# A re-planned DeltaNet and SwiGLU kernel: weight tile sums, masks and K transposes on other engines

## The chip, the cores and the metric

The kernel runs on one core of a Trainium2 chip. Its engines are TensorE (PE in the profile, with PEld for its weight loads), VectorE (DVE), ScalarE (ACT), GpSimd (POOL) and SyncE (SP), which here only issues DMAs. The metric is the device time of one execution in microseconds; three runs of the kernel before gave 681.6, 685.14 and 685.31 us.

## The reference

Two blocks in a row. The first is a DeltaNet recurrence over 768 steps for 4 batches of 8 heads of 48 elements; the second is a feed-forward block with RMS norm over 3072 tokens of 384 elements, 1536 wide inside.

```python
k_n = k / (np.linalg.norm(k, axis=-1, keepdims=True) + 1e-06)
for t in range(S):
    kt, vt, bt = (k_n[:, :, t], v[:, :, t], beta[:, :, t, None])
    y[:, :, t] = np.einsum('bhd,bhde->bhe', q[:, :, t], state)
    v_old = np.einsum('bhde,bhd->bhe', state, kt)
    state = state + bt[:, :, :, None] * np.einsum('bhd,bhe->bhde', kt, vt - v_old)
...
xn = x / np.sqrt(np.mean(x * x, axis=-1, keepdims=True) + 1e-06) * rms_g
g = xn @ w_gate
out = (g * (1.0 / (1.0 + np.exp(-g))) * (xn @ w_val)) @ w_out
```

All is float32, except that the three weight matrices arrive as 64-bit floats and are converted on the chip.

## The kernel before

**Tiling.** The 768 steps are cut into 12 chunks of 64 steps. A chunk holds 256 tokens (4 batches of 64). For each chunk the kernel inverts the coupling of the 64 steps among themselves, so that the recurrence becomes a few matmuls per chunk, and then runs the feed-forward block over the chunk's 256 tokens. The parts are:

- `load`, `norms`, `prep16` (chunks 0 and 1) and `prep` (from chunk 2): K is loaded, normalised (squares on ScalarE at line 665, sum on VectorE, power on GpSimd at 669, scaling of K on GpSimd at 738 or 897), turned on TensorE (`turn`, 621) and multiplied with itself (`scores`, 644). The inverse of the coupling is worked out in small steps on VectorE (816 and 822 for chunks 0 and 1, 977 and 983 later). In `prep` the scores go through DRAM into another layout (`dkk`, `dx`), are scaled on GpSimd (930, 955, 960) or, for chunks 2 and 3, on VectorE, and are put together by two groups of matmuls (1032, 1052).
- `qpart`: Q is turned (on TensorE for chunks 0 and 1, by a transpose on VectorE of a squared layout in `q2` afterwards, 652), multiplied with K (644), and the scores are masked on VectorE into `pt` (689).
- `recur`: the state times K and times Q (`on_state`, 1091, each a group of 64 products on half the rows of the array), then for chunks 0 and 1 the products 1165 and three rounds of 1177 with ScalarE and VectorE between them, and for later chunks one group 1151; then the output (1187) and the state's change (1256). A norm (line 1293, power at 1306) and a transposition (1338, or `dyn` in DRAM and 1329 from chunk 4 on) give the feed-forward block its input.
- `ffn_plain` for chunks 0 and 1 (1405 up, 1387 down); `ffn` from chunk 2 on uses fewer products of sums of operands (1498, with evacuations at 1508, 1510, 1514 and 1515; 1555 down), for which VectorE first works out factors of the weights (1463, 1534).
- `weights`: 18 tiles of 768 KB are loaded into three landing buffers `raw`. ScalarE (561) and VectorE (549, 552, 557) make two parts of each tile, which are added: for the first two tiles (`NPE = 2`) on TensorE, by an identity product of each part into one bank (573, 574) and a copy out on ScalarE (578); for the others by one VectorE add (581).

**Order.** All operations are handed to a planner, `Plan`. It has a duration for each, walks forward and backward over the graph several times (`ROUNDS`, `SEEDS`), and emits the instructions of each engine in the order of its best walk. Operations made while `P.first` is set (the first chunk's preparation and recurrence) have priority over all others. `due(c, lead)` gives the other operations their wanted times, 51 us per chunk. `RELEASE` holds the earliest times of the first weight loads. Until 70 us `filler` puts products of the identity (1664) into TensorE's planned pauses; `supply` models the fetching of TensorE's instructions. There are eight PSUM banks of 128x512, taken and freed in the planned order. TensorE takes products in program order, so one that waits holds up all behind it. Nearly all DMAs are issued on SP's queue by one helper (427).

The masks that the score products are multiplied with:

```python
P.add("DVE", 0.72, lambda d=d, dst=dst: nc.vector.tensor_tensor(
    out=dst, in0=heads(ps[d]), in1=mask_p[:, None, :].to_broadcast([128, 8, C]), op=ALU.mult,
), pr, r=[ps[d], "mask"], w=[("pt", d)], last=ps[d])
```

The way of K through DRAM that `prep` already holds, but never takes, since `KSQ` is 99:

```python
dma(dsq, kn.rearrange("p x e -> p (x e)"), pn, r=kkeys + kp, w=["dsq"], dur=0.6, work=1.4)
for z in range(4):
    src = dsq.rearrange("(gh t) (u z e) -> z t u gh e", t=32, z=4, e=32)[z]
    dst = q2[32 * z : 32 * z + 32].rearrange("p x e -> p (x e)").rearrange("p (u gh e) -> p u gh e", u=8, gh=4)
    dma(dst, src, pn, r=["dsq"], w=q2k[4 * z : 4 * z + 4], work=0.8)
square_turn(kt[ikq], ktk, pr)
```

Of the kernel before, what the change touches and what calls it, by code (L numbers as in the profile page):

```python
# [14 lines left out]
ALU = mybir.AluOpType  # L15
# [3 lines left out]
C = 64  # L19
# [6 lines left out]
ROUNDS, SEEDS = 200, (3,)  # L26
# [3 lines left out]
EARLYN = ()  # L30
RELEASE = (4.7, 13.0, 22.0, 25.0, 30.0, 33.0, 36.0)
KSQ, XSQ = 99, 4
DRAIN, REFILL, GRACE = 0.1, 0.2, 0.0
SHAKE = 0.12
SPARE = 1.0


class Op:
    def __init__(self, eng, dur, fn, prio, deps, lat, acquire, release, slack):
        self.eng, self.dur, self.fn, self.prio = eng, dur, fn, prio  # L40
        self.lat, self.acquire, self.release, self.slack = lat, acquire, release, slack
        self.deps, self.users, self.left = sorted(deps, key=lambda d: d.n), [], len(deps)
        self.mode = None
        self.ready, self.dma, self.ahead, self.work = 0.0, False, 0.0, 0.0
# [24 lines left out]
class Plan:  # L69
# [47 lines left out]
    def forward(self, banks, until):  # L117
# [11 lines left out]
        order, server, end_, mode = [], 0.0, 0.0, 0  # L129
        self.lag = 0.0  # L130
        count, asked, usable = 0.0, -9.0, {}

        def supply(s, dur, n0, size, keep):

            late, last, got = 0.0, asked, {}
            for k in range(int(n0) // BLOCK, int(n0 + size) // BLOCK + 1):
                for mark in (ASKED, LACKED):
                    n = BLOCK * k + mark
                    if not n0 < n <= n0 + size:
                        continue  # L140
                    t = s + late + dur * (n - n0) / size
                    if mark == ASKED:
                        last = max(t + max(REACT, min(server - t + 1.2, 3.5)), last + TURN)
                        got[k + 1] = last + LAND
                    else:
                        late += max(0.0, got.get(k, usable.get(k, 0.0)) - t)
            if keep:
                usable.update(got)
            return late, last
        lanes = [0.0] * 8  # L150
        while len(order) < len(self.ops):
            best = None
            for e in ENGINES:
                for op in cand[e]:
# [12 lines left out]
                    if op.size:  # L167
                        seen += supply(s, op.dur, count, op.size, False)[0]
                    if best is None or (seen, key, op.n) < best[0]:
                        best = (seen, key, op.n), op, s  # L170
# [3 lines left out]
            cand[op.eng].remove(op)  # L174
            for g in op.acquire:
                if not g.taken:
                    g.taken = True
                    free.pop(0)
# [108 lines left out]
def kernel(  # L287
# [58 lines left out]
    NPE, NRAW, NCV = 2, 3, 2  # L346
# [165 lines left out]
    def weights(n0, n1):  # L512
# [14 lines left out]
        for n, (dst, src, keys) in list(enumerate(todo))[n0:n1]:  # L527
# [38 lines left out]
            if n < NPE:  # L566
                width = 768 // parts
                for x_, (a0, a1) in enumerate(((0, 2), (2, 3)) if parts == 3 else ((0, 1), (1, 2))):
# [7 lines left out]
                    P.add("PE", 0.2 + 0.0018 * m, s6, pr, r=cvk + cak + ["ident"], w=[("cvp", n, x_)], ps=ps, size=8)  # L576
# [11 lines left out]
    def load(c, what):  # L588
# [8 lines left out]
        for key, t, src, pr in (("k2", k2[c % NK], k, pk), ("q2", q2, q, pq)):  # L597
            for g in range(2):
                if key[0] not in what or key == "q2" and c > 1:
                    continue  # L600
                dst = t[64 * g : 64 * g + 64, :, 0:D]
                s = src.rearrange("b (y g) t e -> g t (b y) e", g=2)[g, t0 : t0 + C]
                op = dma(dst, s, pr, w=[(key, c % NK, g)] if key == "k2" else q2k[8 * g : 8 * g + 8], dur=0.7, work=1.02, eng="ACT" if c == 0 and g and key == "k2" else "SP", after=((0.0, 12.0, 0.0), (2.2, 40, 0.0))[c]["kqv".index(key[0])] if c < 2 else 44.5)
                op.lat += LATE if c == 1 or key == "q2" else 0.0
# [62 lines left out]

# [9 lines left out]
    def qpart(c):  # L677
# [9 lines left out]
        for d in range(2):  # L687
            dst = pt[:, d:16:2]
            P.add("DVE", 0.72, lambda d=d, dst=dst: nc.vector.tensor_tensor(
                out=dst, in0=heads(ps[d]), in1=mask_p[:, None, :].to_broadcast([128, 8, C]), op=ALU.mult,  # L690
            ), pr, r=[ps[d], "mask"], w=[("pt", d)], last=ps[d])


    def spread_scores(ps, pr, split):
        for d in range(2):
            out_ = scor[:, :, d:16:2].rearrange("p t u -> p u t")
            if split and d == 0:
                P.add("DVE", V(512), lambda o=out_, d=d: nc.vector.tensor_scalar_mul(o, heads(ps[d]), -1.0), pr, r=[ps[d]], w=[("sp", d)], last=ps[d])
            else:
                P.add("ACT", A(512), lambda o=out_, d=d: nc.scalar.mul(o, heads(ps[d]), -1.0), pr, r=[ps[d]], w=[("sp", d)], last=ps[d])  # L700

    def prep16(c):
# [43 lines left out]
        for j in range(3):  # L746
            cut = slice(L * j, L * j + L)
            P.add("ACT", A(256), lambda j=j, cut=cut: nc.scalar.mul(under[:, :, cut], scor[:, cut].rearrange("p t x -> p x t"), below[:, j : j + 1]), pd + (12 if c == 0 else 1), r=[("sp", 0), ("sp", 1), "below"], w=["under"])
# [58 lines left out]
        P.add("DVE", V(128), share1, pi, r=ab, w=xkeys)  # L807
        P.add("DVE", 0.3, share3, pi, r=ab, w=ak)
        P.add("DVE", V(128), share2, pi, r=xkeys, w=ab)
# [27 lines left out]
        P.add("ACT", 0.65, spread, pi, r=ak, w=xkeys)  # L837
# [231 lines left out]
    def recur(c):  # L1069
# [11 lines left out]
        if c:  # L1081
# [27 lines left out]
            P.add("PE", 0.98, lambda: (on_state if c > 1 else on_state_rows)(kt[ikq], psk), pr, r=ktk + sk, w=psk + rk, ps=psk, size=128)  # L1109
# [12 lines left out]
            P.add("PE", 0.98, lambda: on_state(qt, psq), pr, r=qk + sk, w=psq, ps=psq, size=128)  # L1122
# [490 lines left out]
    prep16(0)  # L1613
    qpart(0)
    P.first = False
# [84 lines left out]
```

## Time and profile before

| what | value |
|---|---|
| median of 3 runs | 685.14 us (681.6 to 685.31) |
| the profiled execution | 687.73 us, of it span 686.0 us |
| mean granted TensorE clock | 0.994 |
| VectorE, ScalarE, GpSimd busy | 548.1, 306.5, 137.1 us |
| feed-forward products, chunks 2 to 11 (1498) | 2400 records, 177.2 + 125.9 us |
| their evacuation by adds (1508) | 180 of 682 ns |
| transposes of K on TensorE (621) | 96 records, 13.7 us |
| masks on VectorE (689) | 24, 15.8 us |
| DMA | 58.10 MB, mean 85 GB/s |

The span runs from the first to the last instruction. The profile counts two records for each float32 product, and one for a transposition. Busy times are unions of spans; the spans of matmuls overlap, so that a pause on TensorE is better seen in the starts of its products. A row of the timeline gives the start, the length, the engine, the line, the tiles and the count, and in brackets the idle time of the engine before it and what ended it.

### The profile page before, as it was taken

The page shows a single profiled execution, that of the slowest core. Times are in us where ns is not written, and L with a number is a line of the kernel's source. Part 1 is how long each engine was busy: PE and PEld are TensorE (multiplying, and loading weights), DVE is VectorE, ACT ScalarE, POOL GpSimd, SP SyncE. Part 2 cuts the span into 40 slices and gives each one's busy share as a digit, 9 for nine tenths or more (in the row PEclk, how much of TensorE's full clock was granted, in tenths as well). Part 3 has the DMA queues.
Part 4 walks back from the last instruction along what each step waited for, and adds up shares of the span by engine and source line. Part 5 has one row for each costly group of instructions (what it writes and reads, how often), then busy time and mean ns, then how long its engine had stood idle before and what let it go on. Part 6 is the DMA issues. An engine that isn't in the chain of part 4 may idle for free.

```text
span 686.0 us, 23536 instructions
## 1 busy us (share of the span) xinstructions
PE 667.7 (97%) x10076; PEld 613.7 (89%) x10076; DVE 548.1 (80%) x1153; ACT 306.5 (45%) x717; POOL 137.1 (20%) x142
## 2 busy tenths in 40 slices
PE   7798999999999999999999999999999999999997
PEld 4576778878799999999999999999999999999997
DVE  5749999999989789669888789689689799457473
ACT  6367452434245445336346346256345444253340
POOL 3202030104312312123222222222231301000000
PEclk9899999999999999999999999999999999999999
DMA  8549774614521643643634633643635435002101
GB/s 146 166 109 211 188 229 94 140 26 76 84 49 26 101 71 75 107 80 64 106 58 78 104 66 78 100 82 65 100 60 92 72 79 79 15 12 47 24 1 24
DMA packets 244953, 58.10 MB, mean 85 GB/s; under 512 B 232304, under 2 KB 237424, under 8 KB 244848
## 3 DMA queue, kind: packets, MB, share of 16 engines
q1 hardware_dynamic: 243808, 56.40, 42.6%
q8 instruction: 79, 1.29, 0.8%
q10 hardware_dynamic: 1040, 0.20, 0.2%
q14 instruction: 26, 0.21, 0.1%
HBM read 42.14 MB, written 14.42 MB: 82 GB/s over the span
## 4 chain that ended last, share of the span: by engine, by line
PE 88%; DVE 5%; ACT 2%; issue 2%; DMA 1%; SPq 1%; DVEq 0%; ACTq 0%
PE bank L1498 37%; PE bank L1555 20%; PE bank L1405 8%; PE bank L1387 5%; PE bank L1091 3%; PE bank L644 3%; PE bank L621 2%; PE bank L1187 2%; PE bank L1151 1%; PE bank L1177 1%; SPq L427 1%; DVE tmp L1508 1%; PE bank L1256 1%; PE bank L1032 1%; PE bank L1052 1%
## 5 line engine op out<-in xcount | busy, mean ns | idle before, releaser
L1498 PE MATMUL bank<-xf,w_in 128*128 128x128 f32 x1440 | 177.2, 276 | 0.3 <-ACT tmp L1510 0.3
L1498 PEld LDWEIGHTS bank<-xf,w_in 128*128 128x128 f32 x1440 | 168.7, 192 | 1.8 <-ACT tmp L1510 0.5
L1508 DVE TENSOR_TENSOR tmp<-tmp,bank 128x512 f32<-128x512 f32 x180 | 121.1, 682 | 41.0 <-PE bank L1498 32.3
L1498 PE MATMUL bank<-xf,more 128*128 128x128 f32 x960 | 125.9, 278 | 1.8 <-DVE tmp L1508 1.4
L1498 PEld LDWEIGHTS bank<-xf,more 128*128 128x128 f32 x960 | 115.2, 192 | 4.8 <-DVE tmp L1508 2.0
L1510 ACT COPY tmp<-bank 128x512 f32<-128x512 f32 x120 | 68.9, 585 | 77.0 <-PE bank L1498 60.8
L1514 ACT ACTIVATE tmp<-tmp 128x256 f32<-128x256 f32 x120 | 49.6, 417 | 86.0 <-DVE tmp L1508 85.7
L983 DVE TENSOR_REDUCE acc<-acc 128x30 f32<-128x90 f32 (+4 forms) x150 | 70.9, 473 | 5.2
L669 POOL TENSOR_TENSOR knrm<-ksum,half 128x16 f32<-128x16 f32 x12 | 36.3, 3028 | 166.1 <-DVE ksum L668 166.1
L1555 PE MATMUL bank<-wo_sb,hf 128*128 128x192 f32 x360 | 64.1, 328 | 0.0
L977 DVE TENSOR_TENSOR acc<-acc,at 128x60 f32<-128x60 f32 (+4 forms) x150 | 52.0, 347 | 12.3 <-DMA out_dram<-tmp 4.4
L1555 PEld LDWEIGHTS bank<-wo_sb,hf 128*128 128x128 f32 x360 | 58.3, 190 | 0.4
L1515 DVE TENSOR_TENSOR hf<-tmp 128x256 f32<-128x256 f32 x120 | 48.8, 421 | 9.6 <-ACT tmp L1514 8.5
L930 POOL TENSOR_TENSOR at<-at,beta_b 128x1024 f32<-128x1024 f32 x8 | 19.1, 2384 | 127.4 <-DMA at<-dkk 78.4
L1405 PE MATMUL bank<-xf,w_in 128*128 128x256 f32 x144 | 33.8, 386 | 0.0
L1387 PE MATMUL bank<-wo_sb,hf 128*128 128x384 f32 x96 | 33.7, 490 | 0.0
L1405 PE MATMUL bank<-xp,w_in 128*128 128x256 f32 x144 | 32.8, 380 | 0.0
L1564 DVE TENSOR_TENSOR tmp<-tmp,bank 128x192 f32<-128x192 f32 x30 | 10.5, 350 | 26.4 <-PE bank L1555 26.4
L1405 PEld LDWEIGHTS bank<-xp,w_in 128*128 128x128 f32 x144 | 27.0, 190 | 4.9
L1003 POOL COPY acc<-acc 128x128 f32<-128x128 f32 x40 | 18.1, 480 | 63.3 <-DVE acc L983 62.9
L1405 PEld LDWEIGHTS bank<-xf,w_in 128*128 128x128 f32 x144 | 26.6, 190 | 4.5 <-issue 0.4
L1357 DVE TENSOR_TENSOR xf<-xf 128x256 f32<-128x256 f32 (+1 forms) x70 | 25.1, 396 | 2.6 <-ACT xf L1331 2.0
(203 smaller groups left out, 1030.0 us busy)
## 6 DMA issues: line engine op xcount, KB each, us to landing
at<-dkk SPq DMA_DIRECT2D x20, 256.0 KB, 3.9
more<-in_moe_w_gate_dram SPq DMA_DIRECT2D x6, 768.0 KB, 5.7
vt<-in_v_dram SPq DMA_DIRECT2D x24, 192.0 KB, 4.0
more<-in_moe_w_val_dram SPq DMA_DIRECT2D x6, 768.0 KB, 6.0
more<-in_moe_w_out_dram SPq DMA_DIRECT2D x6, 768.0 KB, 5.1
out_dram<-tmp SPq DMA_DIRECT2D x48, 96.0 KB, 2.2
k<-in_k_dram SPq DMA_DIRECT2D x23, 192.0 KB, 4.1
dyn<-yn SPq DMA_DIRECT2D x16, 192.0 KB, 1.9
```

The source lines that it names most:

```text
L669: P.add("POOL", 2.95, lambda: nc.gpsimd.tensor_tensor(out=knrm[i2], in0=ksum[i2], in1=half, op=ALU.pow), pn, r=[("ksum", i2), "half"], w=[ ...
L977: nc.vector.tensor_tensor(out=acc[:, 1:3, 0:n, j + 2 : W].rearrange("p a i t -> p i a t"), in0=acc[:, old, 0:n, j : j + 2, None].to_broadc ...
L983: nc.vector.tensor_reduce(out=acc[:, new, 0:n, j + 2 : W], in_=acc[:, lo : lo + 3, 0:n, j + 2 : W].rearrange("p a i t -> p i t a"), axis=A ...
L1357: P.add("DVE", V(128 * n), lambda dst=dst, a=a, b_=b_, op=op: nc.vector.tensor_tensor(out=dst, in0=a, in1=b_, op=op), pxv, r=[("xp", 0)], ...
L1387: nc.tensor.matmul(po[p].t[:, 0:DM], hf[:, spot(f), 128 * p : 128 * p + 128], wo_sb[:, spot(f)], start=(f == f0), stop=(f == f1 - 1), skip ...
L1405: nc.tensor.matmul(ps.t[:, TOK * side : TOK * side + TOK], w_in[:, side, h_, 3 * t + i_, n : n + 128], x_[:, 2 * t : 2 * t + 2].rearrange( ...
L1498: nc.tensor.matmul(g.t[:, 128 * z : 128 * z + 128], fac[:, side, 128 * f : 128 * f + 128], xf[:, xs], start=(begin and z == 0), stop=False ...
L1508: P.add("DVE", V(512), lambda t=t, g=g: nc.vector.tensor_tensor(out=t, in0=t, in1=g.t, op=ALU.add), -1, r=[g], w=[tk], last=g)
L1510: P.add("ACT", A(512), lambda t=t, g=g: nc.scalar.copy(t, g.t), -1, r=[g], w=[tk], last=g)
L1514: P.add("ACT", A(256), lambda t=t: nc.scalar.activation(out=t[:, 0:256], in_=t[:, 0:256], func=ACTF.Silu), -1, w=[tk])
L1515: P.add("DVE", V(256), lambda t=t, f0=f0, p=p: nc.vector.tensor_tensor(out=hf[:, spot(f0) : spot(f0) + 2, 128 * p : 128 * p + 128], in0=t[ ...
L1555: nc.tensor.matmul(g.t[:, 0:192], a_[:, f], b_[:, f], start=(begin and f == 0), stop=(f == 5), skip_group_check=True)
```

## The change

The planner gets new rules and constants:

- In a walk after the first, each operation of the first chunk's chain remembers when it started in the walk before. Another operation that would still run at that time on the same engine (with an allowance of 0.1 us) is put behind it.
- The first chunk's Q (`qpart(0)`) is no longer part of that chain.
- The model of instruction fetches also counts the DMA queue before 100 us; several planned durations are changed; fillers leave 0.5 us free, not 1.0; 100 rounds with another seed.

And the kernel does some steps otherwise:

- `NPE = 0`: no tile sums on TensorE; all 18 tiles are added on VectorE.
- `EARLYN = (3, 4)`: weight tiles 3 and 4 land in the space of `hf`, not in `raw`; the loads of tiles 1 to 3 are released at 10, 13 and 16 us, not 13, 22 and 25.
- Both loads of the first Q are issued on ScalarE's queue from 1.4 us on, not on SP's from 12 us on.
- `JKQ = 3`: from chunk 3 on the state's products with K and with Q are one operation of the plan, with four banks.
- `KSQ = 8`: the K of chunks 8 to 11 goes through DRAM into `q2` and is turned by VectorE, not by TensorE.
- `POOLM = 2`: from chunk 2 on ScalarE copies the two banks of Q's scores into `pt`, and GpSimd zeroes what the mask excludes, in two instructions of 64 rows.

```diff
-ROUNDS, SEEDS = 200, (3,)
+ROUNDS, SEEDS = 100, (1,)
...
-EARLYN = ()
-RELEASE = (4.7, 13.0, 22.0, 25.0, 30.0, 33.0, 36.0)
-KSQ, XSQ = 99, 4
+JKQ, JMR, JSC = 3, 99, 99
+EARLYN = (3, 4)
+RELEASE = (4.7, 10.0, 13.0, 16.0, 30.0, 33.0, 36.0)
+KSQ, XSQ = 8, 4
+POOLM = 2
...
-SPARE = 1.0
+SPARE = 0.5
+KEEP, SOON = 0.1, 100.0
...
+        chain = {e: [] for e in ENGINES}
+        for op in self.ops:
+            op.was, op.done = op.start, False
+            if op.first and op.was is not None:
+                chain[op.eng].append(op)
+        for e in ENGINES:
+            chain[e].sort(key=lambda op: -op.was)
...
+                        if t < SOON:
+                            last = max(last, min(server - 0.7, last + 4.5))
...
+                while chain[e] and chain[e][-1].done:
+                    chain[e].pop()
+                kept = chain[e][-1].was + slip if chain[e] else 1e9
...
+                    if not op.first and seen + op.dur - KEEP > kept:
+                        seen = max(seen, kept)
...
+            op.done = True
+            if op.first and op.was is not None:
+                slip = s - op.was
...
-    NPE, NRAW, NCV = 2, 3, 2
+    NPE, NRAW, NCV = 0, 3, 2
...
-                op = dma(dst, s, pr, w=[(key, c % NK, g)] if key == "k2" else q2k[8 * g : 8 * g + 8], dur=0.7, work=1.02, eng="ACT" if c == 0 and g and key == "k2" else "SP", after=((0.0, 12.0, 0.0), (2.2, 40, 0.0))[c]["kqv".index(key[0])] if c < 2 else 44.5)
+                op = dma(dst, s, pr, w=[(key, c % NK, g)] if key == "k2" else q2k[8 * g : 8 * g + 8], dur=0.7, work=1.02, eng="ACT" if c == 0 and (g or key == "q2") else "SP", after=((0.0, 1.4, 0.0), (2.2, 40, 0.0))[c]["kqv".index(key[0])] if c < 2 else 44.5)
...
+            if c < POOLM:
+                P.add("DVE", 0.72, lambda d=d, dst=dst: nc.vector.tensor_tensor(
+                    out=dst, in0=heads(ps[d]), in1=mask_p[:, None, :].to_broadcast([128, 8, C]), op=ALU.mult,
+                ), pr, r=[ps[d], "mask"], w=[("pt", d)], last=ps[d])
+                continue
+            P.add("ACT", A(512), lambda d=d, dst=dst: nc.scalar.copy(dst, heads(ps[d])), pr, r=[ps[d]], w=[("pt", d)], last=ps[d])
+        for g in range(2) if c >= POOLM else ():
+            rows = slice(64 * g, 64 * g + 64)
+            P.add("POOL", 1.9, lambda rows=rows: nc.gpsimd.affine_select(
+                out=pt[rows], in_=pt[rows], pattern=[[0, 16], [1, C]], compare_op=ALU.is_gt, fill=0.0, base=0, channel_multiplier=-1,
+            ), pr, w=ptall)
+            P.ops[-1].port = False
...
-            P.add("PE", 0.98, lambda: (on_state if c > 1 else on_state_rows)(kt[ikq], psk), pr, r=ktk + sk, w=psk + rk, ps=psk, size=128)
+            if c < JKQ:
+                P.add("PE", 0.98, lambda: (on_state if c > 1 else on_state_rows)(kt[ikq], psk), pr, r=ktk + sk, w=psk + rk, ps=psk, size=128)
+            else:
+
+                def both_states():
+                    on_state(kt[ikq], psk)
+                    on_state(qt, psq)
+
+                P.add("PE", 1.96, both_states, pr, r=ktk + qk + sk, w=psk + psq + rk, ps=psk + psq, size=256)
...
-    qpart(0)
     P.first = False
+    qpart(0)
```

## The prediction

> **What bounds the kernel now.** I read the page's busy line first, then the table of windows, then the chain of waits from 27 to 57 us, then the timeline there.
>
> The page's busy line, share of the span in brackets:
>
> ```profile
> PE 667.7 (97%) x10076; PEld 613.7 (89%) x10076; DVE 548.1 (80%) x1153; ACT 306.5 (45%) x717; POOL 137.1 (20%) x142
> ```
>
> Matmuls overlap, so 97% alone proves little. The windows (sum, then busy time of PE, PEld, DVE, ACT, POOL, clock, DMA share, GB/s) show where PE has room:
>
> ```profile
> 30.00:40.00 10.00, 8.39 (x128) 5.79 (x131) 2.46 (x6) 2.74 (x7) 0.00 (x0) 0.83 0.72 151
> 40.00:50.00 10.00, 10.00 (x317) 8.25 (x310) 5.58 (x12) 7.92 (x17) 0.00 (x0) 1.00 0.16 22
> 50.00:60.00 10.00, 8.27 (x128) 6.69 (x119) 9.38 (x29) 9.02 (x28) 1.80 (x2) 1.00 1.05 231
> 140.00:150.00 10.00, 10.00 (x142) 7.84 (x130) 9.79 (x20) 3.35 (x9) 0.00 (x0) 1.00 0.02 5
> 340.00:390.00 50.00, 50.00 (x824) 48.65 (x823) 41.55 (x88) 23.69 (x57) 11.49 (x14) 1.00 0.47 82
> ```
>
> After 190 us TensorE alone binds: VectorE has 8.5 of 50 us free. From 50 to 187 us TensorE and VectorE are both full. From 30 to 50 us VectorE works 8.0 of 20 us and the DMA engines drop to 22 GB/s, although nine weight tiles have to be loaded and converted then. The chain of waits (start, length, what) says why:
>
> ```profile
> 27.76 1.85 PE bank L1165 x64
> 30.09 1.60 issue
> 32.03 1.18 PE bank L573 x2
> 33.21 1.71 PE bank L574 x2
> 34.92 1.39 PE bank L1664 x4
> 36.30 2.00 PE bank L1177 x64
> ```
>
> L1165 and L1177 are the first chunk's recurrence. [...] The timeline shows the second such place, and the first feed-forward matmul:
>
> ```profile
> 43.52 0.30 ACT L1214 COPY u<-bank 128x192 f32<-128x192 f32 x1
> ...
> 46.37 1.07 PE L1177 MATMUL bank<-state,wsum 64*64 64x48 f32 x29
> ...
> 56.53 4.15 PE L1405 MATMUL bank<-xf,w_in 128*128 128x256 f32 x18
> ```
>
> From L1405 on TensorE hardly pauses. So two things can move the end: when L1405 starts, and how much TensorE work follows it.
>
> **The change part by part.**
>
> *Tile sums off TensorE, kept times.* In the built program's order no filler or tile sum stands between these products any more; 22 fillers, for 18, fill other waits. The half-1 values of L1165 were copied out by 30.36 (the timeline's DVE copy L1216, 30.00 + 0.36), and half 0 could have started at 29.6, yet L1177 began at 36.23: 6.6 us lost. At the second place u was ready at 43.82 (43.52 + 0.30) and L1177 began at 46.37: 2.55 lost. Together 9.2 us. The 1.6 us "issue" I cannot tie to the sums, so the gain is 7.6 to 9.2; I take 7.6, since nothing in the diff removes that stall. On VectorE the two sums cost 2 x 0.97 us (the row of L581), inside the 12 us it has idle from 30 to 50; if that cover were gone they would delay the conversions by 1.9.
>
> *What ScalarE pays.* Q of chunk 0 is now issued on ScalarE's queue, ahead of the activation that makes K's squares. K's own issue there took 0.73 us; two are 1.46, less the 0.35 that ScalarE waited for K anyway: +1.1 at the head of the chain. Three things there give it back: the scores of Q (L644, 1.1 us) stood between coupling and L1165 and now sit where fillers stood; a conversion step (L549, 0.57) stood ahead of the diagonal blocks (L854); and Q leaves SP's queue ahead of the weights, where its two issues took 5.16 us. I count this start as 0, with -1 to +1.5. Between the recurrence and L1405, however, the new order puts all three `under` products (L748, 0.73 each) and a 0.37 us copy of chunk 1 before the last scaling of the activations; ScalarE was 90% busy from 50 to 60 us, so about 1.5 us of these lie on the path (0 to 2.6).
>
> So L1405 starts 7.6 - 1.5 = 6.1 us earlier (bounds 9.2 + 1.0 = 10.2 and 7.6 - 1.5 - 2.6 = 3.5).
>
> *Whether the weights follow.* Tiles 3 and 4 get their own landing space in `hf`, and releases move from 22 and 25 to 13 and 16 us, into the slot of 22 GB/s. By the order four tiles are converted before the first feed-forward product; in the trace tile 3 got its last add at 58.52, after L1405. So VectorE stands at the new, earlier L1405 at least where it stood at 56.5. The new wait, that the gated product (L1413) may write `hf` only after tile 3 is read, ends long before.
>
> *Moved behind L1405.* Q of chunk 1: eight transposes (0.87 us at the pace below) and its scores (1.1), 2.0 in all. They partly fill the wait for L867, idle 1.87 us in the trace: I take +1.1 (0 to 2.0).
>
> *Late K by VectorE.* From 459.60 L1498 runs 10.02 us and goes on at 470.49 (rows of the chain): eight transposes take 0.87. Four chunks save 3.5 us of TensorE, and ScalarE eight copies of 0.59. Added per chunk are a store and four loads on SP and a transpose on VectorE (L652, 1.24 us). SP's five issues cost some 2.5 us at the 0.5 of its neighbours; queued behind them are sixteen loads of Q, which share `q2`, and `dyn`/`yn`. Latency: store 1.9, issues 2.0, landing 3.0 (the `dyn` rows), transpose 1.24: 8 us for what took about 2. It is covered while K is early: K's pair of loads issued at 359.79 belongs to a norm whose power starts at 408.86, so K lies ready for tens of us. Price: -3.5, if covered.
>
> *K and Q products as one group.* A lone group of 64-row products costs about 0.33 us beyond its own time (by the starts in the trace the pitch before it is 0.09 longer, the two after it 0.13 and 0.10). Nine joins could save 3.0. But in the built order the feed-forward stage from L1498 on is broken by 55 such groups, before and after: other neighbours were parted. From L1405 on it is 72 against 69, so +1.0 (bounds -3.0 and +1.0). The group now waits for K, Q and state and takes four banks at once, as L1187 with L1256 already does; products of L1498 are queued behind it and L1117 waits for it.
>
> *Mask by GpSimd.* VectorE loses 20 x 0.68 = 13.6 us, ScalarE gets 20 copies of 0.59 = 11.7, GpSimd 20 selects. No row has a select that large: 64x64 took 0.26 us, a memset of 128x1024 1.0, a two-input product of 128x1024 2.38. I take about 1.1 (select and memset both read at most one input), bounds 1.0 and 2.4. On GpSimd's queue they stand ahead of the scalings of K and of the scores (L897, L930), 2.2 us per chunk where it idles 38 of 50. ScalarE and VectorE have room after 190 us too, and the masked scores are wanted only by L1187: 0 on the path, unless GpSimd stops VectorE (a rival below).
>
> Sum: -6.1 + 1.1 - 3.5 + 1.0 = -7.5 us. The profiled execution took 687.73 (span 686.0 and 1.73 around it) and should become 680.2; the median of the runs shown, 685.14, lies 2.6 below it, which gives **677.6 us**.
>
> [...] Two rows bear on sharing between GpSimd and VectorE:
>
> ```profile
> 172.07 0.68 DVE L1463 TENSOR_TENSOR more<-w_in 128x512 f32<-128x512 f32 x1
> ...
> 182.15 4.93 DVE L1463 TENSOR_TENSOR w_in<-w_in 128x512 f32<-128x512 f32 x2
> ```
>
> The same sum takes 0.68 us alone and 2.46 while GpSimd runs a two-input product. Beside GpSimd's one-input copies (L1003) no VectorE instruction was longer than its usual by over 0.22. [...]
>
> **The rivals.**
>
> 1. *VectorE is the bound from 50 to 187 us and the early start is lost there.* For: it is over 98% busy from 120 to 150, and the feed-forward stage of chunk 2 needs all factors. Against: it brings its idle 12 us forward and loses 2 x 2 masks (2.7 us) in this stretch. Then only late K and the switches count: 685.1 - 3.5 + 1.0 = 682.6.
>
> 2. *GpSimd's selects stop VectorE.* Two chunks' selects fall where VectorE is full: 4 x 2.4 = 9.6 us, less the 2.7 saved, is 6.9: 677.6 + 6.9 = 684.5. Against: the L1003 row.
>
> 3. *Late K comes late (slower).* The 8 us path has SP's queue in it, where ten loads of Q took 5.64 us at 342.71. If K lands behind them, TensorE, in order, stands at the scores of K with everything queued behind. 8 + 5.6 - 2 = 11.6 later per chunk, less the 2.7 us between K's scaling (363.44 + 1.65) and its turn at 367.8 that the trace left, is 8.9; over four chunks 35.6: 713. It decides once K's store is issued less than about 8 us before the scores' slot; 13.6 us (8 + 5.6) ahead it would cost nothing even behind Q.
>
> 4. *The grouping does nothing.* By the switch counts I already take it so; were all nine joins real, 677.6 - 4.0 = 673.6.
>
> **How the numbers follow.** A change under 1% (6.9 us) could hardly be told from none, so faster means under 678.3 and slower over 692.0. Forecast (rival 4 within it) 0.68, rival 1 0.14, rival 2 0.08, rival 3 0.10. The forecast's own bounds: 685.1 - 10.2 - 3.5 - 3.0 = 668.4 and 685.1 - 3.5 + 2.0 - 3.5 + 1.0 = 681.1. The centre lies just below the limit, so of 0.68 I give 0.48 to faster and 0.20 to same; rivals 1 and 2 are same. Faster 0.48, same 0.42, slower 0.10. The range must reach rivals 1 and 2: 669 to 685.
>
> **What would show it.** First L1405-type matmul near 50 us, not 56.5; no tile sums; VectorE over 6 of 10 us busy from 30 to 50; 0.87 us gone from the four late K turns, and no TensorE idle before those scores; 20 selects near 1.1 us. It is wrong if the first feed-forward product starts after 53 us, if TensorE idles for weights between 60 and 100 us by more than the 3.2 us it does now (1.87 before L867, 1.32 of "issue" before L644), or if single gaps over 1 us open after 350 us.

## The result, and the profile after

In twenty runs of each, the changed kernel took 686.56 us (median; 684.33 to 695.49) and the kernel before 684.04 (681.48 to 687.48): a ratio of 1.0036, 95% interval 1.0020 to 1.0052. The forecast was 677.6 us, in a range of 669 to 685. By the medians the change costs 2.5 us; it was to save 7.5.

The two profiled executions lie at opposite ends of their kernels' runs: before 687.73 us, after 684.6. Taken by themselves they show a gain. So the kernel before was profiled a second time; that execution took 681.7 (span 680.0). Its windows from 20 to 40 us (sum, busy time of PE, PEld, DVE, ACT, POOL, granted clock, DMA share, GB/s), and the timeline where the feed-forward block begins:

```profile
20.00:30.00 10.00, 7.60 (x214) 6.93 (x215) 9.61 (x21) 5.00 (x12) 5.02 (x2) 1.00 0.51 176
30.00:40.00 10.00, 10.00 (x241) 8.28 (x240) 3.70 (x10) 5.53 (x12) 0.00 (x0) 1.00 0.81 158
```

```profile
51.28 1.16 PE L644 MATMUL bank<-qt,kt 64*64 64x64 f32 x64
52.37 1.99 PE L1405 MATMUL bank<-xf,w_in 128*128 128x256 f32 x8
```

The granted clock, 0.83 from 20 to 40 us in the first profile, is 1.00 here, and the first feed-forward product starts at 52.37, not 56.53. The 4.2 us belong to that execution, not to the program. The comparisons below use this second profile of before, unless they name both.

The changed kernel's page, its windows, and the timeline at its first feed-forward product:

```profile
PE 659.3 (97%) x10036; PEld 607.3 (89%) x10036; DVE 551.5 (81%) x1139; ACT 311.5 (46%) x725; POOL 161.6 (24%) x162
```

```profile
30.00:40.00 10.00, 9.74 (x303) 8.47 (x301) 9.75 (x23) 6.63 (x19) 0.50 (x1) 1.00 0.55 132
40.00:50.00 10.00, 8.76 (x128) 6.61 (x127) 7.43 (x20) 9.07 (x21) 1.55 (x2) 1.00 0.95 195
50.00:60.00 10.00, 9.31 (x166) 7.83 (x164) 9.19 (x20) 6.72 (x17) 1.55 (x1) 1.00 0.34 88
340.00:390.00 50.00, 50.00 (x830) 48.54 (x830) 38.06 (x80) 25.21 (x59) 9.80 (x10) 1.00 0.50 92
390.00:440.00 50.00, 47.04 (x727) 44.99 (x730) 42.96 (x89) 19.66 (x48) 14.98 (x16) 1.00 0.50 93
440.00:490.00 50.00, 47.94 (x774) 46.40 (x767) 40.54 (x89) 23.11 (x55) 15.25 (x15) 1.00 0.54 100
```

```profile
45.55 1.35 PE L1701 MATMUL bank<-ident 128*128 128x512 f32 x4
46.74 1.47 PE L1442 MATMUL bank<-xf,w_in 128*128 128x256 f32 x6
```

Read them from the top. The early start is there: L1442 (L1405 before) starts at 46.74, 5.6 us earlier. VectorE works 17.2 of the 20 us from 30 to 50, where the two profiles of before had 8.0 and 11.6, and the DMA engines move 195 GB/s from 40 to 50 us, where they had moved 22 and 132. But from 390 us on TensorE is no longer full: 47.04 and 47.94 of 50 us, where before it had 50.00. VectorE lost 13.6 us of masks and got two tile sums (1.9 us) and four transposes of K (5.0); from the 548.1 and 555.0 us of the two profiles of before, 541 to 548 were due, and it is busy for 551.5. Something may have made its instructions longer; as those two profiles differ by 7 us themselves, this is a hint and no more.

The accounting that the rest of this document uses is worked out from the starts of TensorE's products in each trace. The span is the start of the first feed-forward product, plus the stretch from there to the last product, plus a tail of 4.4 to 4.9 us. In the stretch, every step from one product to the next that is over 0.3 us longer than the clean pace of that product is a pause; filler products are counted apart; the rest is work.

```text
kernel          first product  pauses  of these after 200 us  fillers  work   span
before, 2nd     52.4            3.7     1.3                   0        619.3  680.0
after           46.7           13.2     9.2                   0        617.9  682.9
```

The parts of a row, with the tail, fall short of the span by up to 0.5 us. So -5.6 from the start and -1.4 of work are outweighed by +9.5 of pauses, nearly all of them (+7.9) after 200 us. The waits of TensorE after 186 us (total us, times, longest) say what they end on; after first, then before:

```profile
PE bank L1535 <- DVE tmp L1545: 6.1, 7, 1.6
PE bank L1119 <- issue: 1.4, 1, 1.4
PE bank L1060 <- DMA m1bd<-dxt: 0.3, 1, 0.3
```

```profile
PE bank L1498 <- DVE tmp L1508: 0.6, 2, 0.4
PE bank L1498 <- issue: 0.3, 1, 0.3
PE bank L1498 <- ACT tmp L1510: 0.3, 1, 0.3
```

TensorE waits for the evacuation L1545 on VectorE. The chain of waits ahead of the longest of these pauses (396.5 us) shows why VectorE is late, although it has 7 of 50 us to spare there:

```profile
383.32 3.69 DMA at<-dkk
...
387.18 2.35 POOL at L958
...
389.59 1.76 POOL acc L983
...
391.84 1.31 POOL at L988
...
393.17 1.14 DVE acc L1005
...
394.62 0.95 DVE acc L1005
...
397.66 0.59 DVE tmp L1545
```

The planner put four pairs of inversion steps (L1005, L1011) ahead of the evacuation. The steps need GpSimd's three scalings (L958, L983, L988), and these need `at`, which two DMAs bring from DRAM. SP's timeline (start, length of the issues) shows eight other issues between the two:

```profile
377.82 0.50 SPq L447 DMA_DIRECT2D at<-dkk  x1
378.37 4.42 SPq L447 DMA_DIRECT2D mt<-dx  x7
382.83 0.45 SPq L447 DMA_DIRECT2D q<-in_q_dram  x1
383.32 0.50 SPq L447 DMA_DIRECT2D at<-dkk  x1
```

So the evacuation, whose products had ended by 396.74 us, stood in VectorE's order behind steps whose data came late: the four pairs run from 393.17 to 397.66, and L1545 starts at 397.58, as the last of them ends. The room was in the engine but not in its order. The late data alone don't make this pause, though: the run with small selects below has the same steps, equally late, in the same place, and TensorE doesn't stand there.

### The profile page after: what moved, and what is told of

Read it like the earlier page. It is cut to its first block, busy times and chain, and to the rows that moved or that the text cites. A ratio compares the mean times of both kernels' runs of the same rounds, so it can differ in the third digit from the quotient of the medians.

```text
span 682.9 us, 23501 instructions
## 1 busy us (share of the span) xinstructions
PE 659.3 (97%) x10036; PEld 607.3 (89%) x10036; DVE 551.5 (81%) x1139; ACT 311.5 (46%) x725; POOL 161.6 (24%) x162
## 4 chain that ended last, share of the span: by engine, by line
PE 62%; DVE 14%; SPq 9%; DMA 7%; issue 3%; POOL 3%; ACT 1%; DVEq 0%; POOLq 0%; ACTq 0%
PE bank L1535 28%; PE bank L1592 12%; SPq L447 9%; PE bank L1442 7%; PE bank L1424 4%; DVE tmp L1545 3%; DMA at<-dkk 2%; DVE acc L1005 2%; PE bank L1119 2%; DVE acc L1011 2%; DMA beta_b<-in_beta_dram 1%; PE bank L1188 1%; DMA q<-in_q_dram 1%; PE bank L1224 1%; PE bank L664 1%
## 5 line engine op out<-in xcount | busy, mean ns | idle before, releaser
L1535 PE MATMUL bank<-xf,w_in 128*128 128x128 f32 x1440 | 181.0, 278 | 3.1 <-DVE tmp L1545 3.0
L1545 DVE TENSOR_TENSOR tmp<-tmp,bank 128x512 f32<-128x512 f32 x180 | 119.3, 681 | 46.4 <-PE bank L1535 36.5
L1535 PE MATMUL bank<-xf,more 128*128 128x128 f32 x960 | 124.4, 278 | 3.1 <-DVE tmp L1545 3.0
L1011 DVE TENSOR_REDUCE acc<-acc 128x30 f32<-128x90 f32 (+4 forms) x150 | 70.9, 472 | 5.2
L1005 DVE TENSOR_TENSOR acc<-acc,at 128x60 f32<-128x60 f32 (+4 forms) x150 | 56.7, 378 | 10.3 <-POOL at L988 7.6
L1552 DVE TENSOR_TENSOR hf<-tmp 128x256 f32<-128x256 f32 x120 | 51.3, 448 | 6.8 <-ACT tmp L1551 6.2
L958 POOL TENSOR_TENSOR at<-at,beta_b 128x1024 f32<-128x1024 f32 x8 | 18.9, 2358 | 106.5 <-DMA at<-dkk 43.7
L1031 POOL COPY acc<-acc 128x128 f32<-128x128 f32 x40 | 20.0, 528 | 98.9 <-DVE acc L1011 77.7
L1442 PE MATMUL bank<-xp,w_in 128*128 128x256 f32 x144 | 33.5, 383 | 1.1 <-DVE hf L1450 1.1
L1442 PE MATMUL bank<-xf,w_in 128*128 128x256 f32 x144 | 33.6, 383 | 0.0
L1442 PEld LDWEIGHTS bank<-xp,w_in 128*128 128x128 f32 x144 | 27.0, 190 | 6.0 <-DVE hf L1450 1.2
L716 POOL TENSOR_SCALAR_AFFINE_SELECT pt<-pt 64x1024 f32<-64x1024 f32 x20 | 24.3, 1216 | 30.2 <-ACT pt L713 29.5
L1442 PEld LDWEIGHTS bank<-xf,w_in 128*128 128x128 f32 x144 | 26.9, 190 | 4.8 <-issue 0.2
```

The source lines that it names most:

```text
L1005: nc.vector.tensor_tensor(out=acc[:, 1:3, 0:n, j + 2 : W].rearrange("p a i t -> p i a t"), in0=acc[:, old, 0:n, j : j + 2, None].to_broadc ...
L1011: nc.vector.tensor_reduce(out=acc[:, new, 0:n, j + 2 : W], in_=acc[:, lo : lo + 3, 0:n, j + 2 : W].rearrange("p a i t -> p i t a"), axis=A ...
L1442: nc.tensor.matmul(ps.t[:, TOK * side : TOK * side + TOK], w_in[:, side, h_, 3 * t + i_, n : n + 128], x_[:, 2 * t : 2 * t + 2].rearrange( ...
L1535: nc.tensor.matmul(g.t[:, 128 * z : 128 * z + 128], fac[:, side, 128 * f : 128 * f + 128], xf[:, xs], start=(begin and z == 0), stop=False ...
L1545: P.add("DVE", V(512), lambda t=t, g=g: nc.vector.tensor_tensor(out=t, in0=t, in1=g.t, op=ALU.add), -1, r=[g], w=[tk], last=g)
L1552: P.add("DVE", V(256), lambda t=t, f0=f0, p=p: nc.vector.tensor_tensor(out=hf[:, spot(f0) : spot(f0) + 2, 128 * p : 128 * p + 128], in0=t[ ...
```

## The experiments

The planner makes a new order for every edit, so each pair of kernels differs by the edit and by the order. Two kinds of runs get around this: edits that leave the order of every engine as it is (`tiny_select`, `late_k_free`), and runs of one kernel with several seeds. The planner also works out when its own order should end; that figure ("timetable") is the kernel's, not a measurement.

**The three later parts undone one by one, and all together.**

```diff
 no_late_k:   -KSQ, XSQ = 8, 4              +KSQ, XSQ = 99, 4
 no_gp_mask:  -POOLM = 2                    +POOLM = 99
 no_join:     -JKQ, JMR, JSC = 3, 99, 99    +JKQ, JMR, JSC = 99, 99, 99
 plan_only:   all three
```

> K of chunks 8 to 11 is turned by TensorE again, without the way through DRAM; all else stays, and the planner makes its order anew. If late K makes the pauses that TensorE has after 390 us (about 8 us beyond its clean pace), they go and 3.5 us of transposes come back: about 4.5 us less than the changed kernel, 682 us (ratio to the kernel before 0.997). If GpSimd's selects make them, they stay and the transposes are added: 690 us (1.009). If it is chance of the planner's order, the pauses change place and size in no fixed way, within some 3 us of 686.6 on either side.

> The mask is VectorE's product again, with no copy by ScalarE and no select; all else stays, and the planner makes its order anew. If the selects (20 of 1.2 us ahead of the scalings on GpSimd's queue) make the pauses after 390 us, they go: 678.5 us (0.992). If they only stretch VectorE's steps, some 2 to 4 us go: 683 to 685. If late K makes the pauses, nothing goes, and VectorE has 13.6 us more to do where it has 8 of 50 us free: 686 to 689 (1.003 to 1.007).

> The state products of K and Q are two groups again; all else stays, and the planner makes its order anew. If joining saves nothing (the count of small groups within the feed-forward products hardly differs), 685 to 688 us (0.999 to 1.006). If each of nine joins saves 0.33 us, 3 us more: 689.6 (1.008). If the joined group, which waits for K, Q and state at once, makes the pauses: up to 8 us less, 679 (0.993).

> Late K, the select and the joined products are all undone; what stays is the new start (no tile sums on TensorE, kept times, earlier landing of tiles 3 and 4, Q of chunk 0 issued by ScalarE) and the new planner settings. If the start is worth what the profile shows at the first feed-forward product (9.6 us earlier, less 1.1 for what moved behind it) and the three other parts gave it back, 684.0 - 8.5 = 675.5 us (0.988). If the early start is lost between 50 and 187 us because VectorE is full there, 684 (1.000). If every new plan has its own pauses, anything between: 676 to 687.

Measured against before (ratio, interval): without late K 690.37 us (1.0097, 1.0077 to 1.0118), without GpSimd's mask 692.49 (1.0131, 1.0108 to 1.0154), with separate products 688.04 (1.0079, 1.0049 to 1.0110), with the new start alone 690.41 (1.0097, 1.0072 to 1.0121). Every part that was taken out made the kernel slower, and taking out all three did not bring 675.5 but 690.4. None of the three parts is "the" culprit by this; and the start, taken alone, looked some 7 us worse than before. Its windows say where:

```profile
20.00:30.00 10.00, 7.28 (x116) 6.17 (x116) 6.90 (x17) 3.84 (x8) 5.02 (x2) 0.83 0.65 243
30.00:40.00 10.00, 8.97 (x258) 8.18 (x257) 9.83 (x22) 5.04 (x13) 0.00 (x0) 1.00 0.75 209
40.00:50.00 10.00, 7.96 (x149) 6.19 (x144) 3.91 (x8) 5.82 (x18) 1.75 (x2) 0.66 0.55 72
```

The granted clock drops twice, and the first feed-forward product starts at 53.43. `no_gp_mask` shows the same drop at 40 us (start 53.12); `no_late_k` and `no_join` do not (48.84 and 46.54), but have 11.1 and 8.4 us of pauses. `no_gp_mask` and `plan_only` lie above everything that was expected of them (689 and 687 at most). `no_late_k` lies outside the 3 us that it gave to chance and at the 690 that it gave to the selects, but with its pauses in other places. The orders differ too much to read an edit's worth from these four: that pauses change "in no fixed way" fits them best, though more widely than was expected.

**Before, once more and with other seeds; after with the seed of before.**

```diff
 before_seed1:  -ROUNDS, SEEDS = 200, (3,)   +ROUNDS, SEEDS = 100, (1,)
 before_s8:     -ROUNDS, SEEDS = 200, (3,)   +ROUNDS, SEEDS = 200, (8,)
 after_seed3:   -ROUNDS, SEEDS = 100, (1,)   +ROUNDS, SEEDS = 200, (3,)
```

> The kernel before, unchanged, for a second profile. In the first one the granted clock fell to 0.72 and 0.74 of full speed between 20 and 35 us and the span was 686.0 us. If that drop belongs to that execution, it is absent here, the first feed-forward product starts about 4.4 us earlier than 56.5 us (686.0 less the 681.6 that most executions show), at about 52, and the span is 681 to 682. If the drop belongs to the kernel, it is here again.

> The kernel before with the changed kernel's seed and number of rounds alone (seed 1, 100 rounds, for seed 3 and 200), so the work is the same and only the planner's order is another. If the order that the planner happens to find decides, this is slower than before by several us: its own timetable ends at 689.1 us where that of the kernel before ends at 677.8, so up to 695 us (1.016). If the chip evens such differences out, 684 to 686 (1.000 to 1.003).

> The changed kernel with the seed and rounds of the kernel before (seed 3, 200 rounds). Its own timetable ends at 673.5 us, 0.7 later than the changed kernel's. If the timetable tells the time, 687 us (1.0045). If chance of the order counts for more than the timetable shows, anything from 682 to 692; the two of seed 1 and seed 3 differing by over 2 us would show it.

> The kernel before with seed 8 in place of seed 3 (200 rounds as before): the same work in another order. Its own timetable ends at 688.1 us, 10.3 later than that of the kernel before; seed 1 ended at 689.1 and took 702. If the kernel before owes its time to a lucky seed, this is near 700 us (1.024), at least over 692. If seed 1 was the odd one, it is 684 to 687 (1.000 to 1.005).

The second profile of before is told above. With the changed kernel's seed and rounds the kernel before took 702.0 us (1.0268, 1.0230 to 1.0307; at most 695 had been expected), with seed 8 695.02 (1.0163, 1.0129 to 1.0198). The work is the same to the instruction; only the order differs. The waits of TensorE from 100 to 640 us, of seed 1 and of seed 8:

```profile
PE bank L1091 <- DVE state L1369: 9.0, 1, 9.0
PE bank L1498 <- ACT tmp L1510: 3.6, 1, 3.6
```

```profile
PE bank L1405 <- DVE hf L1413: 6.6, 1, 6.6
PE bank L1387 <- DVE hf L1413: 2.3, 1, 2.3
```

One wait of 9.0 us in one order and one of 6.6 in the other, both on VectorE between 100 and 190 us, where it is full. The order of seed 3 has no such wait (3.7 us of pauses in the whole stretch). In seed 1 the granted clock is also 0.50 from 112 to 124 us, and the work is 625.4 us, not 619.3; whether the wait of 9.0 us brought that drop the run doesn't show. So against these two orders the kernel before owes 11 to 18 us to its own, and the diff gives this order up in its first line. By the planner's own reckoning seed 3 is the best of the seeds 1 to 12 for the kernel before (677.8, where the twelve spread up to 689.4). The two orders that were run stand at the slow end of this spread (688.1 and 689.1); four others end under 682.

The changed kernel with seed 3 took 684.72 us (1.0031, 1.0016 to 1.0047), level with seed 1. Its order is not one that a second draw mends.

**The selects made small, the order kept.**

```diff
-    out=pt[rows], in_=pt[rows], pattern=[[0, 16], [1, C]], compare_op=ALU.is_gt, ...
+    out=pt[rows, 0:1], in_=pt[rows, 0:1], pattern=[[0, 1], [1, C]], compare_op=ALU.is_gt, ...
```

> The changed kernel in its own order, with GpSimd's select cut from 64x1024 elements to 64x64, so the masked scores keep their upper triangle (only the first of 16 heads is masked). If the selects delay GpSimd's scalings or stretch VectorE's first steps beside them (0.22 us became 1.13 at 393.17), the pauses of TensorE after 186 us shrink from 9 us to under 5, and the time from 686.6 to 682 (0.997). If the selects cost nothing on the path, 686 to 687 and the pauses stay.

681.56 us (0.9977, 0.9954 to 1.0000). Against the changed kernel's 1.0036 that is 0.0059, or 4.0 us (about 2 to 6 by the two intervals). Pauses fall from 13.2 to 8.8. TensorE's waits after 186 us with the small selects:

```profile
PE bank L1535 <- DVE tmp L1545: 2.3, 5, 0.8
PE bank L1060 <- DVE tmp L1545: 0.9, 1, 0.9
PE bank L1119 <- issue: 0.8, 1, 0.8
PE bank L664 <- DVE kt L672: 0.3, 1, 0.3
```

How they cost that much shows, for the longest pause, in VectorE's first inversion steps ahead of it, with the full selects and with the small ones:

```profile
393.17 1.13 DVE L1005 TENSOR_TENSOR acc<-acc,at 128x60 f32<-128x60 f32 x1 [1.26 <-POOL at L988]
394.33 0.26 DVE L1011 TENSOR_REDUCE acc<-acc 128x30 f32<-128x90 f32 x1
394.62 0.94 DVE L1005 TENSOR_TENSOR acc<-acc,at 128x112 f32<-128x112 f32 x1
```

```profile
392.83 0.23 DVE L1005 TENSOR_TENSOR acc<-acc,at 128x60 f32<-128x60 f32 x1 [1.20 <-POOL at L988]
393.09 0.26 DVE L1011 TENSOR_REDUCE acc<-acc 128x30 f32<-128x90 f32 x1
393.38 0.28 DVE L1005 TENSOR_TENSOR acc<-acc,at 128x112 f32<-128x112 f32 x1
```

Two selects run from 393.09 to 395.44 beside them. A two-input step of 0.23 us takes 1.13, one of 0.28 takes 0.94; the one-input reduce between them keeps its 0.26. GpSimd releases the first step and in the same moment starts the selects that hold it up. The selects' row, and what TensorE does next, with the full selects and with the small ones:

```profile
393.09 2.35 POOL L716 TENSOR_SCALAR_AFFINE_SELECT pt<-pt 64x1024 f32<-64x1024 f32 x2
...
398.31 1.16 PE L1535 MATMUL bank<-xf,w_in 128*128 128x128 f32 x8 [1.57 <-DVE tmp L1545]
```

```profile
395.40 2.17 PE L1535 MATMUL bank<-xf,w_in 128*128 128x128 f32 x16
```

The two steps together are 1.56 us longer, and TensorE stands for 1.57; with the small selects it runs on, although the first step had waited 1.20 us for GpSimd there too. Whether the other pauses shrink for the same reason, or because the full selects also hold up GpSimd's own queue, this run doesn't separate.

**Late K's loads freed of its store, the order kept.**

```diff
-    dma(dsq, kn.rearrange("p x e -> p (x e)"), pn, r=kkeys + kp, w=["dsq"], ...
+    dma(dsq if c == KSQ else dsr, kn.rearrange("p x e -> p (x e)"), pn, r=kkeys + kp, w=["dsq"], ...
```

> The changed kernel in its own order; the stores of late K of chunks 9 to 11 go to a second scratch array, so their loads do not wait for the store (they bring chunk 8's K again, so the output is not the reference's). If the way of late K through DRAM is on the path (1.9 us of store per chunk and more), 3 chunks gain up to 6 us: 681 (0.995). If late K is covered, as VectorE's single wait of 0.4 us for it says, 686 to 687 (1.002 to 1.005).

687.33 us (1.0050, 1.0026 to 1.0074): no gain. In the changed kernel's trace the late K tile is hardly waited for: VectorE stood once for its loads, and TensorE once for the transpose.

```profile
its engine sat idle before it (us, times) until:
  DMA q<-dsq: 0.4, 1
who waited for it (us, times):
  PEld bank L664: 0.2, 1
```

The wait for the store is covered, and it is not what makes the pauses. What late K's further issues on SP's queue and its transposes on VectorE do to the order isn't tested by this run.

**Other orders of the new start alone, and of the change with VectorE's mask.** Only `ROUNDS, SEEDS` of `plan_only` and `no_gp_mask` are changed, to `200, (5,)` and `200, (8,)` for the first and to `200, (2,)` and `200, (9,)` for the second.

> The kernel with only the new start and planner settings (690.4 us at seed 1), with seed 5 and 200 rounds: its timetable ends at 674.6 us in place of 680.6. If the order that a seed finds is what held that kernel back, it loses about those 6 us: 684.4 (1.0006), and with the 6.2 us that the kernel before needs beyond its own timetable 681 (0.996). If the new start itself is what costs 6 us, 690 again (1.009).

> The changed kernel with VectorE's mask (692.5 us at seed 1), with seed 2 and 200 rounds: its timetable ends at 673.8 us in place of 677.7. It has no selects, which cost the changed kernel 4 us by the run with small ones. If the order held it back: 688.6 by its own excess over the timetable of seed 1 (14.8), 680 by that of the kernel before (6.2). If VectorE's 13.6 us of masks are on the path, it stays over 690 whatever the order.

> The kernel with only the new start and planner settings, with seed 8 and 200 rounds (its timetable ends at 675.1 us). Seed 1 took 690.4 and had the granted clock drop twice before 50 us, seed 5 took 677.6 without a drop. If the new start is worth its 5.7 us in an ordinary order, this is 677 to 682 (0.991 to 0.998). If seed 5 was the lucky one, it is 686 to 691 (1.004 to 1.011).

> The changed kernel with VectorE's mask, with seed 9 and 200 rounds (its timetable ends at 675.3 us). It has the new start, late K and the joined products; seed 1 took 692.5 and seed 2 681.1. If late K and the joined products are worth their 2.8 us of TensorE work beside the new start alone, this is below the run with seed 8 of the new start alone: 675 to 680. If they bring as many pauses as they save, it is level with that run or above it: 680 to 686.

```text
kernel                      seed  timetable  median   ratio (95%)             first product  pauses  work
before                      3     677.8      684.04   1                       52.4            3.7    619.3
                            8     688.1      695.02   1.0163 (1.0129-1.0198)  54.1           14.3    621.2
                            1     689.1      702.0    1.0268 (1.0230-1.0307)  54.1           17.5    625.4
new start alone             5     674.6      677.58   0.9912 (0.9880-0.9943)  46.6            2.7    621.6
                            8     675.1      685.61   1.0039 (1.0014-1.0063)  47.0            5.6    621.9
                            1     680.6      690.41   1.0097 (1.0072-1.0121)  53.4            6.0    621.2
after, VectorE masks        9     675.3      681.05   0.9983 (0.9960-1.0007)  44.8            8.8    618.3
                            2     673.8      681.13   0.9961 (0.9938-0.9984)  47.2            8.9    618.7
                            1     677.7      692.49   1.0131 (1.0108-1.0154)  53.1           12.6    618.9
after                       3     673.5      684.72   1.0031 (1.0016-1.0047)  46.8            9.5    620.9
                            1     672.8      686.56   1.0036 (1.0020-1.0052)  46.7           13.2    617.9
```

(Medians are of separate sessions, in which the kernel before had medians of 682.3 to 684.0; ratios are to the runs of before in the same session. First product, pauses and work are of the one profiled execution; fillers behind the first product, 0 to 1.9 us, are left out.)

The new start with seed 5 is the fastest kernel of the study: 677.58 us, faster than both by 0.6 to 1.2% (before) and about 1.2% (after). All of TensorE's waits that its profile names from 100 to 640 us:

```profile
PE bank L1535 <- issue: 1.1, 1, 1.1
PE bank L1535 <- ACT tmp L1547: 0.3, 1, 0.3
```

The same code spans 13 us over three seeds, before 18, the change with VectorE's mask 11; the two orders of the changed kernel differ by under 2. With seed 2 the change with VectorE's mask took 681.13 us, so VectorE's masks alone don't keep it over 690. Seed 8 of the new start came out just under the range that its expectation had given to "seed 5 was the lucky one" (685.61), with runs from 682.84 to 689.81; so one good order does not settle what the start is worth in an ordinary one. What the table does show is that the new start brings the first product to 45 to 49 us in every order in which the clock didn't drop, and that late K and the joined products together take some 3 us of TensorE's work away in all three orders with VectorE's mask (618.6 on average against 621.6), but not in the changed kernel's seed 3 (620.9), and that neither has to show in the time. `no_gp_mask_s9`, at 681.05 level with before, settles nothing: it is faster than the new start's seed 8, as it should be if the 3 us count, and slower than its seed 5, with 8.8 us of pauses against 2.7. Whether these two parts bring pauses of their own stays open.

## Why the prediction was wrong, point by point

**Start.** Forecast -6.1 us (bounds 3.5 to 10.2), measured -5.6 against the undisturbed profile (46.74 and 52.37). The term holds, but in part by luck, since its working leaned on a disturbed stretch: the 6.6 us "lost" around the tile sums were read where the clock stood at 0.83. In the second profile that place loses 3.1 us (L1165 ends at 28.95, L1177 starts at 32.05), without the 1.6 us of "issue"; the same working would then have given about -4.2 us. Taking the median 2.6 us below the profiled time had allowed for part of this.

**The weights follow.** They do: VectorE is busy 9.75 and 7.43 us in the two windows from 30 to 50, against the "over 6 of 10" asked for (the second profile of before has 3.70 and 7.91, so only the first window is a sign), and pauses between the first product and 200 us are 4.0 us against 2.4. Rival 1 (the start lost between 50 and 187) would have eaten 5.0; 1.6 went that way.

**TensorE's work.** Forecast +1.1 - 3.5 + 1.0 = -1.4, measured -1.4 (617.9 and 619.3). To the tenth this is luck: with seed 3 the changed kernel's work is 620.9, so an order alone moves it by 3.0. Late K's transposes are gone from TensorE (64 records for 96), and rival 3 (late K late) did not happen: waits of 0.4 and 0.2 us, and nothing gained by freeing the loads. Of the joined products no saving was forecast; by the one pair of orders the work grows by 2.4 us without them (620.3 and 617.9), no more than an order can move it. Rival 4 had named this case; whether joining brings it in other orders too wasn't tried.

**Masks: the step that failed.** The prediction put the selects at "0 on the path, unless GpSimd stops VectorE" and gave that rival 8 in 100, because beside GpSimd's one-input copies (L1003) no VectorE instruction had been longer by over 0.22 us. Those copies are short (median 0.41 us), and among the instructions that were 0.22 longer are ones with two inputs in SBUF: L1463 at 164.88 took 0.90 for 0.68, two of L1515 0.64 for 0.42. The row held against the rival showed the same lengthening at a small size. The duration was right (1.22 us mean, forecast 1.1). The path was not: with the selects made small and nothing else moved, 4.0 us go, and VectorE's busy time falls from 551.5 to 539.5 us, which is where its 13.6 us of saved masks went. Matched instruction by instruction, VectorE's are 13.0 us longer with the full selects, 10.2 of these in instructions that a select overlaps; by line it is 5.1 in L1005, 2.6 in L1552 and 2.4 in L1394, all with both inputs in SBUF (1.6 more are in L1500, beside no select). The rival's price (4 selects at 2.4 us where VectorE is full, before 190 us) named the wrong place: the cost falls after 200 us, where the steps are queued ahead of evacuations. One line of the diff bears on this, and the prediction passed over it: `P.ops[-1].port = False` behind the select. With `port` the planner marks operations of VectorE that read no PSUM bank and operations of GpSimd other than powers, and doesn't start one engine's before the other's has ended; the selects are exempted, so nothing in the plan keeps them off the steps that they stretch. The kernel with the mark left on wasn't run.

**"ScalarE and VectorE have room after 190 us too": the same step, in its second half.** Room in an engine was taken for room in its order. The longest pause (1.57 us of waiting before 398.31) opened where late and lengthened steps stood in front of an evacuation that TensorE waited for, and that follows from the order, not from the share of busy time. The prediction's own sign of failure, "single gaps over 1 us open after 350 us", is what happened (1.74 us at 396.5, 1.39 at 454.5, 1.09 at 554.9). With the small selects 5.3 us of pauses after 200 us remain, 4.0 more than in before; which single edit makes these, if any does, the runs don't say. So of the 9 us between the forecast (677.6) and the result (686.56) the selects are 4.0; for the rest the cause stays open.

**What wasn't in the sum at all.** `ROUNDS, SEEDS` stands in the first lines of the diff and was priced at nothing, by silence. On the kernel before, a change there costs 18 us (seed 1) or 11 (seed 8), by the ratios. The forecast compared two designs; the runs compare two draws, of which the one before was the best of twelve by the planner's own reckoning. Shown is that the order alone moves each of three kernels by 11 to 18 us, and that the new start in one order reaches 677.58 us, the forecast's figure, without late K, selects or joined products. Not shown is what each part is worth on average over orders: three draws of a kernel are too few for that.

## What to carry to other kernels

Where a planner or scheduler orders the instructions, a diff's first effect is a new order; run the kernel before with two or three other seeds before believing any difference smaller than their spread, and test an edit's own cost with one that leaves the order as it is. Spare time of an engine in a window says nothing of a wait in it: look at which instruction stands ahead of the one that the critical engine waits for, how late its data can come, and what can lengthen it. And take a second profile when the profiled execution isn't near the median: here the first one had 4.2 us of its own at the start.

## What the runs showed of the hardware

GpSimd's select reads one input, and still stretches VectorE: the two-input steps of L1005 by up to 0.9 us each (0.23 to 1.13), the group's mean from 344 to 378 ns. The evacuations L1545, with one operand in a PSUM bank, keep their mean (681 ns with the full selects, 682 with the small ones; the four that start at 465.36, beside the selects at 465.13, take 2.47 us together), and the reduces L1011 theirs (472 and 473). A step with one input isn't always spared: L572, a TENSOR_SCALAR of 128x768, took 1.35 us beside two full selects (at 95.23) and 0.55 in the other run. In these rows, VectorE's steps and GpSimd's selects in the run with the full selects, then VectorE's steps with the small ones:

```profile
L1005 DVE TENSOR_TENSOR acc<-acc,at 128x60 f32<-128x60 f32 (+4 forms) x150 | 56.7, 378 | 10.3 <-POOL at L988 7.6
...
L716 POOL TENSOR_SCALAR_AFFINE_SELECT pt<-pt 64x1024 f32<-64x1024 f32 x20 | 24.3, 1216 | 30.2 <-ACT pt L713 29.5
```

```profile
L1005 DVE TENSOR_TENSOR acc<-acc,at 128x60 f32<-128x60 f32 (+4 forms) x150 | 51.6, 344 | 9.0 <-POOL at L988 7.4
```

Why the two-input steps grew, and L572 with them, no run here shows. The prediction had looked at the number of GpSimd's inputs instead (2.46 us for 0.68 beside a two-input product, at most 0.22 more beside a one-input copy).

The granted clock between 20 and 50 us is not a property of the program alone. In one profile of the kernel before it fell to 0.83 in two windows of 10 us, in the other it stayed at 1.00; the longest pause of TensorE ahead of the drop was 2.0 us in both. In the first profile it is 0.50 from 22.19 to 25.60 us and from 32.43 to 35.84. In the order of `plan_only` it fell in the profile, and the mean clock of all six runs was 0.990 to 0.995; with seed 5 it was 0.997 to 1.000 in all six. The first feed-forward product comes 4.2 us later with the drop in the one kernel (56.5 and 52.4), and 6.8 later in the other's two orders (53.4 and 46.6), which differ in more than the clock. The two drops of the first profile are 3.41 us long each; why one program met them in one execution and not in the other, these views don't show.
